# MLP phase of a fused attention and MLP kernel: one more output accumulator, one side accumulator less, an earlier load, and small vector work spread over units

## The chip, the core and the metric

The kernel runs on one core of one Trainium2 chip. The metric is the device time of one execution in microseconds (us), as a median over several runs. Profiles and traces come from single executions. A profile's span is about 1.8 us shorter than the device time of the same execution, so spans are compared with spans and times with times.

Names: TensorE is PE in profile lines, VectorE is DVE, ScalarE is ACT, GpSimd is POOL.

## The reference, cut to what matters

Part A is attention with a recurrent memory over 64 segments; part B is layer norm, two matrix products and a gelu, for each of 2048 rows. Gates mix the two.

```python
def _B_ref(x, w1, b1, w2, b2):                 # x (1, 2048, 512), w1 (512, 1376), w2 (1376, 512)
    y = _layernorm(x, axis=-1)
    h = _gelu(jnp.einsum('bsd,df->bsf', y, w1) + b1)
    return jnp.einsum('bsf,fd->bsd', h, w2) + b2
g = _sigmoid((x * gate_w).sum(-1, keepdims=True))
a = _A_ref(x, A_mem0, A_Wq, A_Wk, A_Wv, A_Wo, A_seg_len)     # the attention, unchanged here
b = _B_ref(x, B_w1, B_b1, B_w2, B_b2)
return g * a + (1 - g) * b
```

## The kernel before

The MLP comes first, then the attention. The 16 tiles of 128 rows form 8 blocks of two. The hidden width of 1376 makes 11 pieces, so the MLP is a loop over 88 units. Unit `(blk, fc)` does one up-projection (four matmuls, then a gelu on ScalarE), and the down-projection of the unit two earlier (two matmuls into two accumulators, one for each tile). Statistics, norms and gate products of later tiles run beside it on VectorE. In the last three blocks, a generator (`setup`) puts one step of the attention's first projections into each unit; these use "side" banks.

```python
    ld_x(0, 1); ld_x(1, 2)
    nc.sync.dma_start(w1_sb[:, :, 0:3 * P], w1_src[:, :, 0:3 * P])
    ...
    ld_w2(0, 4)
    nc.sync.dma_start(w1_sb[:, :, 3 * P:F], w1_src[:, :, 3 * P:F])
    ld_w2(4, FCF)
    ...                                          # rest of w2, b2, m0
    ld_x(2, 4)
    ld_x(4, 8)
    ...
    def side(shape, dtype=FP32):                 # two side banks in turn
        side_n[0] += 1
        while side_n[0] - 2 in side_todo:
            flush(dve_q)
            flush(act_q)
        return bank(5 + side_n[0] % 2, shape, dtype)

    def stats(t0, t1, act=False):                # for each tile: bn_stats, bn_aggr; then
        ...                                      # 12 small Newton steps for 1/sqrt(var + eps)
    def gates(t0, t1):                           # z = sum(x * gate_w), one instruction a tile
        ...
    def gates2(t0, t1):                          # tanh on ScalarE, then g and 1 - g on VectorE
        ...
    def up(u):                                   # hp: two banks
        hp = mps.tile([P, TB * P], FP32, tag="hp", bufs=2, name="hp")
        ...                                      # 4 matmuls, then the gelu on ScalarE
    def down(u, hg_):
        ...
            if fc == 0:
                bpt[T] = mps.tile([P, Dm], FP32, tag=f"bp{T % 3}", name="bp")    # three accumulators
            nc.tensor.matmul(bpt[T][:], lhsT=..., rhs=w2_sb[:rows, fc, :], start=(fc == 0), stop=(fc == FC - 1))
        if fc == FC - 1:                         # the first of the pair is emptied on VectorE,
            nc.vector.tensor_scalar(out=c_all[:, T, :], in0=bpt.pop(T)[:], scalar1=omg_all[:, T:T + 1], ...)
            c_q.append(T + 1)                    # the second later on ScalarE (c_act)
    ...
    for u in range(NBLK * FC):
        blk, fc = divmod(u, FC)
        T1 = (blk + 1) * TB
        pend.append((u, up(u)))
        c_act()
        if len(pend) > LAG:                      # LAG = 2
            down(*pend.pop(0))
        if T1 < NT:
            if fc == 1 or fc == 3:
                ys[fc // 2] = norm(T1 + fc // 2)
            elif fc == 4 or fc == 6:
                norm_tr(T1 + fc // 2 - 2, ys[fc // 2 - 2])   # transposes on TensorE, copy to yT on VectorE
        if blk % 2 == 0:
            G = 2 * blk
            if fc == 4 and G + 8 <= NT:
                stats(G + 4, G + 8)              # four tiles in one burst
            if fc == 7:
                gates(G, G + 4)                  # four tiles in one burst
        elif fc == 0:
            gates2(2 * blk - 2, 2 * blk + 2)
        ...
        if blk >= NBLK - 3:
            next(pre, None)                      # one step of setup
```

## Time and profile before

| | before |
|---|---|
| device time, median of 3 runs | 851.37 us (849.81 to 851.44) |
| span of the profile | 848.8 us |
| TensorE busy | 813.2 us, 96% |
| up-projection of block 2 starts | 38.36 us |
| MLP phase ends (last `c_all` eviction starts on ScalarE) | 115.20 us |

A wait line reads "who, line, waited for whom: us in total, times, longest". A timeline line reads "start, duration, engine, line, operation, tiles, shape, count", and in brackets the idle time of that engine before it and what ended it.

### The profile page before, as it was taken

What the parts mean: (1) busy time and instruction counts of PE and PEld (TensorE: products, weight loads), DVE (VectorE), ACT (ScalarE), POOL (GpSimd) and SP (SyncE); (2) the same over time, 40 slices, a digit from 0 to 9 for tenths busy, and PEclk for the clock granted to TensorE, in tenths of its full rate; (3) what the DMA queues carried; (4) which work ended last, traced back from release to release, by engine and by line L of the source; (5) the groups of instructions that cost most, each with busy time, mean ns of one, the idle gap of its engine ahead of it and who ended that gap; (6) DMA issues with size and microseconds to landing.
All of it is one profiled execution on the core that took longest, in us unless ns stands there. A gap on an engine that the chain in (4) does not pass through costs nothing.

```text
span 848.8 us, 49249 instructions
## 1 busy us (share of the span) xinstructions
PE 813.2 (96%) x22417; PEld 495.7 (58%) x22417; DVE 502.4 (59%) x1017; ACT 434.2 (51%) x1244; POOL 275.2 (32%) x625
## 2 busy tenths in 40 slices
PE   4989999999999999999999999999999999999986
PEld 2655455566656666556666665656665666656554
DVE  4555335666665666565666566666656566657553
ACT  2444454555545554555455555555454545555552
POOL 8000123333233424242424342333324342424220
PEclk8999999999999999999999999999999999999999
DMA  9890221010101010101000000101010101010000
GB/s 317 268 361 8 65 63 27 4 35 4 35 10 35 4 34 12 34 12 30 15 22 24 19 26 17 29 10 35 10 35 7 34 9 36 9 31 9 10 4 24
DMA packets 38216, 37.64 MB, mean 44 GB/s; under 512 B 13545, under 2 KB 36434, under 8 KB 36466
## 3 DMA queue, kind: packets, MB, share of 16 engines
q1 hardware_dynamic: 37874, 34.31, 12.3%
q8 instruction: 177, 2.90, 1.4%
q14 instruction: 37, 0.30, 0.1%
q0 software_dynamic: 128, 0.13, 0.1%
HBM read 26.03 MB, written 6.29 MB: 38 GB/s over the span
## 4 chain that ended last, share of the span: by engine, by line
PE 90%; DVE 6%; issue 1%; DMA 1%; SPq 1%; ACT 1%; DVEq 0%; ACTq 0%
PE b L210 34%; PE b L232 17%; PE b L221 17%; PE b L383 5%; PE hp L454 3%; PE bp L471 3%; PE b L359 2%; PE b L368 2%; PE b L660 1%; PE b L695 1%; PE b L388 1%; PE b L649 1%; DVE st L401 1%; DVE junk L422 1%; DMA Wo_sb<-in_A_x_dram 1%
## 5 line engine op out<-in xcount | busy, mean ns | idle before, releaser
L216 DVE STREAM_TRANSPOSE Tt<-b 128x512 f32<-128x512 f32 (+1 forms) x384 | 225.6, 613 | 79.1 <-PE b L210 65.4
L210 PEld LDWEIGHTS <-hT 128*32 128x32 bf16 x5120 | 134.8, 97 | 100.0 <-DVE hT L696 15.7
L232 PE MATMUL b<-Wo_sb,UTT 128*32 128x256 bf16 (+1 forms) x4736 | 162.7, 285 | 1.2 <-ACT UTT L595 0.8
L221 PE MATMUL b<-Wv_sb,hT 128*32 128x512 bf16 x2048 | 141.9, 378 | 0.0
L210 PE MATMUL b<-Wq_sb,hT 128*32 128x512 bf16 x2048 | 133.0, 379 | 1.4 <-DVE hT L696 1.4
L210 PE MATMUL b<-Wk_sb,hT 128*32 128x256 bf16 (+1 forms) x3072 | 133.4, 308 | 0.0
L232 PEld LDWEIGHTS <-UTT 128*32 128x32 bf16 x4736 | 121.3, 97 | 19.6 <-ACT UTT L595 1.5
L630 ACT CAST KT<-Tt 128x256 bf16<-128x256 f32 (+1 forms) x192 | 87.1, 476 | 53.6 <-DVE Tt L216 53.5
L581 POOL TENSOR_TENSOR Px<-E,R 128x256 bf16<-128x256 bf16 x64 | 43.1, 673 | 219.0 <-DVE R L665 219.0
L665 DVE RECIPROCAL R<-b 128x256 f32<-128x256 f32 x64 | 112.5, 1757 | 0.0
L630 POOL CAST QT<-Tt 128x512 bf16<-128x512 f32 x64 | 39.3, 614 | 192.3 <-DVE Tt L216 192.3
L595 ACT CAST UTT<-b 128x256 bf16<-128x256 f32 x256 | 76.8, 386 | 23.6 <-PE b L388 23.1
L684 ACT CAST wsb<-b 128x256 bf16<-128x256 f32 x66 | 24.6, 373 | 120.0 <-PE b L232 120.0
L653 DVE RECIPROCAL R<-b 128x64 f32<-128x64 f32 x64 | 35.6, 557 | 79.1 <-PE b L650 79.1
L630 ACT CAST QT<-Tt 128x512 bf16<-128x512 f32 x64 | 39.6, 619 | 67.6 <-DVE Tt L216 67.6
L459 ACT ACTIVATE hg<-hp,b_sb 128x256 bf16<-128x256 f32 x80 | 37.6, 473 | 54.1 <-PE hp L454 54.1
L383 PEld LDWEIGHTS <-V 32*128 32x128 bf16 x4096 | 35.2, 91 | 46.5 <-DVE Pm L655 32.4
L221 PEld LDWEIGHTS <-hT 128*32 128x32 bf16 x2048 | 49.5, 96 | 21.1
L664 ACT CAST UTT<-b 128x64 bf16<-128x64 f32 x128 | 20.9, 215 | 75.6 <-PE b L388 75.6
L454 PE MATMUL hp<-yT,w_sb 128*128 128x256 bf16 (+1 forms) x352 | 55.8, 284 | 2.5 <-DVE yT L444 2.5
L583 POOL TENSOR_TENSOR racc<-racc,R 128x320 f32<-128x320 f32 x64 | 55.6, 868 | 0.0
L471 PE MATMUL bp<-w_sb,hg 128*128 128x512 bf16 x160 | 50.0, 392 | 3.7 <-DVE c_all L474 3.7
(116 smaller groups left out, 1046.5 us busy)
## 6 DMA issues: line engine op xcount, KB each, us to landing
Wv_sb<-in_A_Wv_dram SPq DMA_DIRECT2D x4, 1024.0 KB
Wq_sb<-in_A_Wq_dram SPq DMA_DIRECT2D x4, 1024.0 KB
Wk_sb<-in_A_Wk_dram SPq DMA_DIRECT2D x4, 1024.0 KB
Wo_sb<-in_A_Wo_dram SPq DMA_DIRECT2D x2, 2048.0 KB
vd<-vt SPq DMA_DIRECT2D x32, 128.0 KB
vs<-vd SPq DMA_DIRECT2D x256, 16.0 KB
out_dram<-o SPq DMA_DIRECT2D x16, 128.0 KB
Wo_sb<-in_A_x_dram SPq DMA_DIRECT2D x1, 1024.0 KB
```

The source lines that it names most:

```text
L210: nc.tensor.matmul(bk[32 * j:32 * j + 32, 0:n], lhsT=G[:, kc, :], rhs=W5[t][:, kc, h0:h1, j, :], start=(kc == 0), stop=(kc == KC - 1), til ...
L216: nc.vector.transpose(out=Tt[:, 0:n], in_=bk[:, 0:n])
L221: nc.tensor.matmul(bk[32 * j:32 * j + 32, :], lhsT=G[:, kc, :], rhs=Wv5[:, kc, 4 * vb:4 * vb + 4, j, :], start=(kc == 0), stop=(kc == KC - ...
L232: nc.tensor.matmul(bk[32 * g:32 * g + 32, :], lhsT=ut[:, i, j, c0:c0 + 32], rhs=Wo_sb[:, 4 * i + j, d0:d1], start=(j == 0 and i < 4), stop ...
L383: nc.tensor.matmul(U[j][:, i, :], lhsT=V[q, i, :], rhs=Pt[q, i, c_main:c_main + n], start=(i == 0), stop=False, skip_group_check=True, til ...
L454: nc.tensor.matmul(hp[:rows, :], lhsT=w1_sb[:, kc, fc * P:fc * P + rows], rhs=yTs[blk][:, kc, :], start=(kc == 0), stop=(kc == KC - 1))
L471: nc.tensor.matmul(bpt[T][:], lhsT=hg_[:rows, tt * P:(tt + 1) * P], rhs=w2_sb[:rows, fc, :], start=(fc == 0), stop=(fc == FC - 1))
L581: nc.gpsimd.tensor_tensor(out=Px[:, :, 0:32], in0=E[:, :, 16:48], in1=Rr, op=ALU.mult)
L583: nc.gpsimd.tensor_tensor(out=racc[:], in0=racc[:], in1=R[:], op=ALU.add)
L595: nc.scalar.copy(out=UTT[T % 2][:, :, j, c0 + M:c0 + 40], in_=U[:])
L630: (nc.gpsimd.tensor_copy if bi == 2 else nc.scalar.copy)(out=dst, in_=Tv)
L665: nc.vector.reciprocal(out=R[:, 8 * NG:].rearrange("p (i q) -> p i q", q=32), in_=sr)
```

## The change

The intent is to take TensorE's waits out of the MLP phase. Each tile of a block and of the next gets its own accumulator, paid for with one of the two side banks. x of block 1 is loaded ahead of w2. Statistics and gates are dealt out one tile to a unit. Two smaller moves go with it: the transposes come one unit later, and `c_act` (the ScalarE eviction) runs once a block. The diff is cut, and some short lines are joined.

```diff
     nc.gpsimd.dma_start(gw_bc[:], gate_w.partition_broadcast(P))
+    ld_x(2, 4)
     ld_w2(0, 4)
 ...
-    ld_x(2, 4)
     ld_x(4, 8)
 ...
-    pools["nTt"] = 2
+    pools.update(nTt=2, nside=1)                 # side(): nside banks in turn; 2 again in the attention
 ...
-                bpt[T] = mps.tile([P, Dm], FP32, tag=f"bp{T % 3}", name="bp")
+                bpt[T] = mps.tile([P, Dm], FP32, tag=f"bp{T % 4}", name="bp")
 ...                                               # setup: one more step after each tile's eviction
             flush(act_q)
-        left_v_in(0)
+            yield
 ...
                 flush(dve_q)
+                yield
+        left_v_in(0)
 ...
-    stats(0, 2, act=True)
+    bn(0); bn(1); root_act(0, 2)
 ...
-    stats(2, 4)
+    bn(2); bn(3); newton(2, 4)
 ...
-        c_act()
+        if fc == 2:
+            c_act()
 ...
-            elif fc == 4 or fc == 6:
+            elif fc == 5 or fc == 7:               # norm_tr
 ...
         if blk % 2 == 0:
-            G = 2 * blk
-            if fc == 4 and G + 8 <= NT:
-                stats(G + 4, G + 8)
-            if fc == 7:
-                gates(G, G + 4)
-        elif fc == 0:
-            gates2(2 * blk - 2, 2 * blk + 2)
+            if fc in (2, 5, 6, 7) and T1 + 2 < NT:
+                bn(T1 + 2 + (2, 5, 6, 7).index(fc) )
+            if fc == 8 and T1 + 2 < NT:
+                newton(T1 + 2, T1 + 6)
+        elif fc in (2, 4, 6, 8):
+            T = T1 + (fc - 2) // 2
+            if T < NT:
+                gates(T, T + 1)
+        elif fc == 10 and T1 < NT:
+            gates2(T1, T1 + 4)
+        if blk == 0 and fc in (9, 10):
+            gates(fc - 9, fc - 8)
+        if blk == 1 and fc == 0:
+            gates2(0, 2)
+        if blk == 1 and fc in (1, 3):
+            gates(2 + fc // 2, 3 + fc // 2)
+        if blk == 1 and fc == 9:
+            gates2(2, 4)
```

More of the change, by code (lines that the diff above doesn't have):

```diff
@@ L195, in side @@
         side_n[0] += 1
-        while side_n[0] - 2 in side_todo:
+        n = pools["nside"]
+        while side_n[0] - n in side_todo:
             flush(dve_q)
             flush(act_q)
-        return bank(5 + side_n[0] % 2, shape, dtype)
+        return bank(5 + side_n[0] % n, shape, dtype)
     Wq5 = Wq_sb[:].rearrange("p k (h j e) -> p k h j e", h=H, j=4)
@@ L394, with bn, root_act, newton @@
     I32 = mybir.dt.int32
-    def stats(t0, t1, act=False):
-        n = t1 - t0
-        for T in range(t0, t1):
-            st = mwork.tile([P, nc.vector.BN_STATS_DIM], FP32, tag="st", bufs=4, name="st")
-            nc.vector.bn_stats(out=st[:], in_=x_all[:, T, :])
-            nc.vector.bn_aggr(out=mv_all[:, T, :], in_=st[:])
-        if act:
-            nc.scalar.activation(out=rstd_all[:, t0:t1], in_=mv_all[:, t0:t1, 1], func=ACTF.Sqrt, bias=eps_t[:], scale=1.0)
-            nc.vector.reciprocal(out=rstd_all[:, t0:t1], in_=rstd_all[:, t0:t1])
-            return
+    def bn(T):
+        st = mwork.tile([P, nc.vector.BN_STATS_DIM], FP32, tag="st", bufs=4, name="st")
+        nc.vector.bn_stats(out=st[:], in_=x_all[:, T, :])
+        nc.vector.bn_aggr(out=mv_all[:, T, :], in_=st[:])
+    def root_act(t0, t1):
+        nc.scalar.activation(out=rstd_all[:, t0:t1], in_=mv_all[:, t0:t1, 1], func=ACTF.Sqrt, bias=eps_t[:], scale=1.0)
+        nc.vector.reciprocal(out=rstd_all[:, t0:t1], in_=rstd_all[:, t0:t1])
+    def newton(t0, t1):
+        n = t1 - t0
         ve = mwork.tile([P, n], FP32, tag="ve", name="ve")
@@ L508 @@
     nc.vector.memset(eps_t[:], LN_EPS)
-    stats(0, 2, act=True)
+    bn(0)
+    bn(1)
+    root_act(0, 2)
     nc.scalar.activation(out=warm[:], in_=eps_t[:], func=ACTF.Gelu_apprx_tanh)
@@ L513 @@
     norm_tr(1, ys[1])
-    stats(2, 4)
+    bn(2)
+    bn(3)
+    newton(2, 4)
     pre = setup()
@@ L558 @@
     cw = loop.enter_context(tc.tile_pool(name="cw", bufs=2))
-    pools.update(ps=pb, sb=cw, nTt=3)
+    pools.update(ps=pb, sb=cw, nTt=3, nside=2)
     man = tc.manual_schedule()
```

## The prediction

> **What bounds the kernel now.** I read the page's busy shares and the chain that ended last first, to see which engine sets the time, then the waits of TensorE in the first 155 us, then the timelines of TensorE, VectorE and ScalarE in the stretch that the diff touches.
>
> ```profile
> span 848.8 us, 49249 instructions
> PE 813.2 (96%) x22417; PEld 495.7 (58%) x22417; DVE 502.4 (59%) x1017; ACT 434.2 (51%) x1244; POOL 275.2 (32%) x625
> ...
> PE 90%; DVE 6%; issue 1%; DMA 1%; SPq 1%; ACT 1%; DVEq 0%; ACTq 0%
> ```
>
> TensorE is busy 96% of the span and is 90% of the chain. The diff touches only the MLP phase, which ends at about 115.2 us (its last down-projections, a chain piece "PE bp L471 x6", run from 113.87 for 1.31 us). The remaining 733 us, the recurrent attention, have the same instructions before and after. So the question is how much TensorE idles before 115 us. Its waits there (window 0 to 155 us):
>
> ```profile
> PE tp L443 <- DVE y L436: 10.5, 2, 5.7
> PE bp L471 <- DVE c_all L474: 3.7, 3, 1.6
> PE hp L454 <- DVE yT L444: 2.5, 3, 1.0
> ...
> PE tp L443 <- DVE yT L444: 0.5, 1, 0.5
> ```
>
> The timeline of TensorE alone puts them in time:
>
> ```profile
> 13.71 0.59 PE L471 MATMUL bp<-w_sb,hg 128*128 128x512 bf16 x2
> 19.12 0.61 PE L443 MATMUL tp<-ident,y 128*128 128x128 bf16 x4 [4.81 <-DVE y L436]
> ...
> 30.75 0.38 PE L471 MATMUL bp<-w_sb,hg 128*128 128x512 bf16 x1 [1.20 <-DVE c_all L474]
> ...
> 49.66 0.61 PE L454 MATMUL hp<-yT,w_sb 128*128 128x256 bf16 x4 [1.00 <-DVE yT L444]
> ...
> 53.83 0.38 PE L471 MATMUL bp<-w_sb,hg 128*128 128x512 bf16 x1 [1.61 <-DVE c_all L474]
> ...
> 72.73 0.61 PE L454 MATMUL hp<-yT,w_sb 128*128 128x256 bf16 x4 [1.00 <-DVE yT L444]
> ...
> 76.91 0.38 PE L471 MATMUL bp<-w_sb,hg 128*128 128x512 bf16 x1 [0.88 <-DVE c_all L474]
> ```
>
> Three kinds. The first, 4.81 us, is TensorE waiting for the normed rows of tiles 2 and 3. The waits on c_all (1.20, 1.61, 0.88) are a down-projection that needs a third accumulator while VectorE has not emptied the old one. The waits on yT (1.00, 1.00) are the next block's first up-projection. Two smaller ones (a pair of down-projections at 40.54 and 63.61 shows 0.73 in place of 0.59) add 0.13 each. After 77 us there is none until the phase ends. What lies behind each is in the timeline of VectorE:
>
> ```profile
> 14.48 0.69 DVE L401 BATCH_NORM_STATS2 st<-Wo_sb 128x6 f32<-128x512 bf16 x1 [6.63 <-DMA Wo_sb<-in_A_x_dram]
> ...
> 49.18 0.42 DVE L444 COPY yT<-tp 128x512 bf16<-128x512 bf16 x1
> 49.52 0.68 DVE L422 SCALAR_TENSOR_TENSOR junk<-Wo_sb,gw_bc 128x512 bf16<-128x512 bf16 x1
> ...
> 53.02 0.75 DVE L474 TENSOR_SCALAR c_all<-bp,omg_all 128x512 bf16<-128x512 f32 x1
> ```
>
> The first wait is a transfer: x of tiles 2 and 3 lands at 14.48, behind all of w1 and w2; statistics and Newton steps follow until 18.65. The later ones are bursts: between 43.60 and 49.27 VectorE does four statistics and one Newton chain without a break, so the copy of yT comes at 49.18; then four gate products stand before c_all at 53.02.
>
> **What the Trainium skill says.** "TensorE: Matmul & The Clock Gate", Part 1, says that the array runs at half rate until it was busy for a window of about 3.4 us, and falls back after an idle one. The trace agrees: one unit (four up-matmuls, two down-matmuls) has a pitch of 1.71 us after the 4.81 us wait (19.52 to 21.23) and of 0.87 us later (24.40 to 25.27), and the granted clock reads 0.50 from 17 to 23 us. The same page (Part 1, "Architectural detail") calls the queues of ScalarE and VectorE strict FIFO; the bursts above show it, as the yT copy waits behind Newton steps that it does not need. "DMA: Bandwidth & Descriptors", "Queues, rings and completion order", says that an engine consumes descriptors in ring order; it fits x(2,4) landing last. "Perfetto Trace Analysis", "Optimization Strategy", says that consistent bubbles can mean too few buffers; the c_all waits, once in every second block, are of that kind.
>
> **The change, part by part.** *(a) x of tiles 2 and 3 ahead of w2.* Its 256 KB now come after 640 KB (x of tiles 0, 1 and the first w1 part), not after some 3,000 KB. From the DMA rates by slice (about 87, 177, 332 GB/s in the first three slices of 2.9 us) I estimate a landing at 7.8 us. VectorE is free at 7.85 (it has just copied the second yT), and from the first statistic to the norm took 18.65 - 14.48 = 4.17 us, so norm(2) is ready to start at 12.0, not 18.65. The rest of w1 is pushed back by 256 KB at some 370 GB/s (the mean of the two slices there, 388 and 351), about 0.7 us: it landed at 11.40 (TensorE waited for it 0.83), so now at 12.1.
>
> *(b) The new wait in block 0.* The statistic of tile 4 now stands in VectorE's queue at unit 2, ahead of norm(3). Its x is in the 512 KB that still follow the weights: the bytes ahead are the same as before, so it lands 512 KB / 400 GB/s = 1.3 us after 14.48, at 15.9 (estimate). From there by durations of the trace (pitch of one statistic with its aggregate 0.80, norm 0.40, copy 0.40, Newton 2.35, gate 0.74): statistic 4 to 16.7, norm(3) 17.1, copy(2) 17.5, statistics 5 and 6 19.1, copy(3) 19.5, statistic 7 20.3, Newton 22.7, gates of tiles 0 and 1 to 24.2. TensorE meanwhile, at half rate up to about 13.3 and 0.87 a unit after, with 0.22 for each transpose group, finishes block 0 at 20.4 and unit 13 at 22.95. Then it stops: the tanh for the gates sits in ScalarE's FIFO after the gelu of unit 11, waits for z until 24.2, and holds back the gelu of unit 12, whose hp buffer unit 14 needs. 24.2 + 0.2 (tanh) + 0.47 (gelu) = 24.9: a wait of 1.95 us. This chain from x(4,8), not TensorE, sets the time here; a TensorE up to 1.95 us later changes nothing.
>
> Remaining block 1: eight units of 0.87 and two transpose groups, 7.4 us, and 0.4 for the second transpose, since VectorE, still catching up with the gates of tiles 2 to 7, copies yT(4) only at 29.85. Block 2 starts at 24.9 + 7.4 + 0.4 = 32.7. Before, it started at 38.36. **Gain so far 5.7 us**: 4.81 of wait, 2.1 of half clock after it (4.2 us at half rate) and 1.20 of c_all wait go, about 0.7 for w1 and the two new waits come.
>
> *(c) Four accumulators and spread work, blocks 2 to 7.* With four banks a block's two accumulators are needed again only two blocks on, 10 us after their last matmul, so the eviction is never in the way: 0.13 + 1.61 + 0.13 + 0.88 = 2.75 us go. VectorE's work in an even block is now 0.75 + 2 x 0.40 + 4 x 0.80 + 2 x 0.42 + 2.35 = 7.9 us in a block of 10.0 (11 x 0.87 + 2 x 0.22); the copy of the second yT stands behind three statistics, not behind Newton, and is done three units before it is needed. An odd block has 0.75 + 0.80 + 4 x 0.74 + 0.84 + 0.33 = 5.7 us. So the two yT waits of 1.00 go as well. **4.75 us.**
>
> *(d) One side buffer in place of two.* Costs a bank (4 + 2 + 1 + 1 = 8). The added yields put one unit, 1.30 us in this stretch (77.55 to 78.85), between the last matmul into the side bank and the first into the next; the eviction takes 0.71 on VectorE or 0.58 on ScalarE. Setup needs 31 steps and a last one, of 33 units. 0 us. The late copy of VL (1.04 us on GpSimd) ends about when the phase does and is first needed in the attention of step 0: 0 us.
>
> Sum: 5.7 + 4.75 = 10.4 us. 851.4 - 10.4 = **841.0 us**.
>
> **The rivals.** *Everything hides:* if TensorE never waited after the change, the upper bound is 4.81 + 2.1 + 1.20 + 4.75 = 12.9 us, 838.5. For it speaks an x(4,8) that lands near 14; against it the equal bytes ahead of it. *The tile-4 statistic waits longer:* if Wv's transfers, issued from 8.68, share the rings with x(4,8), it lands at 18 and each us is lost directly: 843 to 844. Against it speaks ring order. *The side bank becomes a wait:* if each of seven evictions came 0.5 late, 3.5 us are lost, 844.5; against it the 1.30 us unit. *VectorE becomes the bound* in even blocks: at 7.9 of 10.0 us it would need work that I have missed; one us per block would give 847. *The clock does not rise at 13.3* because of the 0.8 us hole for w1: up to 1.7 us of TensorE time, but inside the 1.95 of slack, so nothing.
>
> **Range and chances.** The removable idle time is 12.9 us, 1.5%, so over 2% (below 834.3) would need something in the attention, where nothing changed. The rivals that cost lie between 1 and 6 us, and the runs before spread by 1.6. Eight in ten: 838 to 845. Faster by over 2%: 0.03; within 2%: 0.95; slower: 0.02.
>
> **What would show it.** Right: no wait on y of 4.8 us in TensorE's list, and the granted clock not back at 0.50 near 17 to 23 us; one wait of 1 to 2 us for ScalarE near 23 us; VectorE idle until about 16 us on a transfer of x; no c_all or yT waits of 0.9 or more from 33 us on; the phase's last down-projection ending near 104.8 in place of 115.2; attention as long as before within 1 us. Wrong: a new wait on the side bank between 65 and 100 us, repeated waits of TensorE on yT in even blocks, or an attention part that differs by more than 2 us.

## More of the kernel before

Line numbers of the kernel before and of the changed one differ (the up-projection is L454 before and L456 after).

The end of the MLP phase is this line (timeline of ScalarE, kernel before):

```profile
115.20 0.69 ACT L479 ACTIVATE c_all<-bp,omg_all 128x512 bf16<-128x512 f32 x1 [0.83 <-PE bp L471]
```

## The result

| | before | changed |
|---|---|---|
| device time, median of 4 runs each | 851.40 us | 838.42 us (837.94 to 839.50) |
| ratio changed / before | | 0.9849 (0.9828 to 0.9870) |
| span of the profile | 848.8 us | 836.5 us |
| up-projection of block 2 starts | 38.36 us | 32.33 us |
| MLP phase ends | 115.20 us | 103.73 us |

A ratio is the mean time of one kernel's fast runs over the mean of the other's fast runs of the same rounds, so it is not quite the ratio of the medians. The gain is 13.0 us (1.5%), within the predicted range and at its fast end; 10.4 us were predicted. It is even just past the prediction's "upper bound" (838.5, TensorE never waiting), although TensorE still waited; the part on why the prediction was right says how.

The page of the changed kernel: busy shares, then the chain that ended last.

```profile
PE 810.3 (97%) x22404; PEld 495.3 (59%) x22417; DVE 502.4 (60%) x1019; ACT 434.2 (52%) x1245; POOL 274.4 (33%) x625
...
PE 93%; DVE 3%; DMA 1%; SPq 1%; issue 1%; ACT 1%; DVEq 0%; ACTq 0%
```

VectorE's busy time is the same, 502.4 us. Its share of the chain fell from 6% to 3%: the same work stands in other places.

TensorE's waits in the first 155 us of the changed kernel (those in the attention are left out):

```profile
PE tp L445 <- DVE y L438: 5.7, 1, 5.7
...
PE hp L456 <- DMA w_sb<-in_B_w_dram: 0.7, 1, 0.7
PE tp L445 <- DVE yT L446: 0.5, 1, 0.5
PE hp L456 <- DVE yT L446: 0.5, 1, 0.5
PE hp L456 <- ACT hg L461: 0.5, 1, 0.5
```

The first line is the start of the kernel, which was there before as half of the 10.5 us on `y`. The other half, 4.81 us, is gone, and so are all waits on `c_all` and the two of 1.00 on `yT`. Two small ones are new: 0.7 on w1, and 0.5 on a gelu of ScalarE. Here is where they lie (timelines of TensorE, VectorE and ScalarE of the changed kernel):

```profile
12.21 1.03 PE L456 MATMUL hp<-yT,w_sb 128*128 128x256 bf16 x4 [0.71 <-DMA w_sb<-in_B_w_dram]
...
24.94 0.60 PE L456 MATMUL hp<-yT,w_sb 128*128 128x256 bf16 x4 [0.51 <-ACT hg L461]
```

```profile
16.14 0.69 DVE L399 BATCH_NORM_STATS2 st<-Wo_sb 128x6 f32<-128x512 bf16 x1 [3.44 <-DMA Wo_sb<-in_A_x_dram]
```

```profile
24.32 0.20 ACT L427 ACTIVATE th_all<-z_all 128x2 f32<-128x2 f32 x1 [1.49 <-DVE junk L424]
24.43 0.82 ACT L461 ACTIVATE hg<-hp,b_sb 128x256 bf16<-128x256 f32 x2
...
103.73 0.69 ACT L481 ACTIVATE c_all<-bp,omg_all 128x512 bf16<-128x512 f32 x1 [0.83 <-PE bp L473]
```

VectorE stands for 3.44 us until x of tile 4 lands at 16.14. From there statistics, Newton steps and two gate products run on it without a break until 24.3; the tanh on ScalarE waits for the second gate, and the two gelus behind it come late. The last line is the end of the MLP phase.

The 12.3 us between the two spans split into 6.0 up to the start of block 2, 5.4 in blocks 2 to 7, and 0.8 after the MLP phase.

### The profile page after: what moved, and what is told of

It reads as the page before. It is cut to its first block, busy times and chain, and to the rows that moved or that the text cites. A ratio compares the mean times of both kernels' runs of the same rounds, so it can differ in the third digit from the quotient of the medians.

```text
span 836.5 us, 49240 instructions
## 1 busy us (share of the span) xinstructions
PE 810.3 (97%) x22404; PEld 495.3 (59%) x22417; DVE 502.4 (60%) x1019; ACT 434.2 (52%) x1245; POOL 274.4 (33%) x625
## 3 DMA queue, kind: packets, MB, share of 16 engines
q1 hardware_dynamic: 37874, 34.31, 12.3%
## 4 chain that ended last, share of the span: by engine, by line
PE 93%; DVE 3%; DMA 1%; SPq 1%; issue 1%; ACT 1%; DVEq 0%; ACTq 0%
PE b L211 35%; PE b L233 18%; PE b L222 17%; PE b L384 5%; PE hp L456 4%; PE bp L473 4%; PE b L360 2%; PE b L369 2%; PE b L681 2%; PE b L716 1%; PE b L389 1%; PE b L670 1%; DMA Wo_sb<-in_A_x_dram 1%; PE b L320 1%; PE b L373 0%
## 5 line engine op out<-in xcount | busy, mean ns | idle before, releaser
L717 DVE CAST hT<-b 128x32 bf16<-128x32 f32 x63 | 12.1, 192 | 61.8 <-PE b L716 61.8
```

## The experiments

The theory put to the test had four claims: (1) after the change, the chain from the landing of x of tiles 4 to 7 over VectorE to the tanh sets when block 2 starts; (2) waits do not add up, since one that is removed uncovers the next; (3) it is the order of VectorE's work, not the number of accumulators, that made the `c_all` waits of blocks 2 to 7; (4) the single side bank is free because of the added steps. The rivals were additive waits, TensorE alone as the bound of the head, and the fourth bank as the cure. Claim (3) goes against the attribution in the prediction.

All results in one table. "x at 4" is when VectorE starts the statistic of tile 4 after waiting for its x. The column "blocks 2-7" is the end of the MLP phase minus the start of block 2, all from the profiles. Times and ratios of the experiments are of 4 or 5 runs beside 9 runs of the kernel before on the same chip (of the changed kernel, 4 beside 4); every output of the experiments was correct.

| run | x at 4 | block 2 starts | MLP ends | blocks 2-7 | time, us | ratio to before (95%) |
|---|---|---|---|---|---|---|
| before | | 38.36 | 115.20 | 76.84 | 851.40 | |
| changed | 16.14 | 32.33 | 103.73 | 71.40 | 838.42 | 0.9849 (0.9828 to 0.9870) |
| e1_x_early_only | 15.98 | 34.38 | 111.24 | 76.86 | 847.90 | 0.9962 (0.9948 to 0.9975) |
| e2_x_late | | 36.44 | 107.83 | 71.39 | 842.51 | 0.9902 (0.9887 to 0.9917) |
| e3_three_acc | 16.00 | 33.11 | 104.91 | 71.80 | 841.08 | 0.9884 (0.9869 to 0.9899) |
| e4_four_acc_bursts | 16.31 | 33.99 | 110.13 | 76.14 | 844.96 | 0.9929 (0.9916 to 0.9943) |
| e5_gates_in_gap | | 31.36 | 102.76 | 71.40 | 834.96 | 0.9817 (0.9803 to 0.9830) |
| e6_w1_split | 16.71 | 32.79 | 104.19 | 71.40 | 838.68 | 0.9855 (0.9840 to 0.9870) |
| e7_both | | 29.90 | 101.30 | 71.40 | 835.68 | 0.9823 (0.9809 to 0.9836) |
| e8_x48_late | 19.57 | 35.63 | 107.03 | 71.40 | 840.45 | 0.9878 (0.9863 to 0.9893) |
| e9_no_added_steps | 15.89 | 32.07 | 105.08 | 73.01 | 839.69 | 0.9868 (0.9850 to 0.9885) |
| e10_gap_three_acc | 16.05 | 31.29 | 103.08 | 71.79 | 837.20 | 0.9844 (0.9827 to 0.9860) |
| after_again | 16.89 | 32.97 | 104.37 | 71.40 | 837.43 | 0.9844 (0.9828 to 0.9860) |
| before_again | | 38.44 | 115.29 | 76.85 | 850.52 | 0.9998 (0.9984 to 1.0012) |

### The early load alone (e1)

```diff
 # kernel before
+    ld_x(2, 4)
     ld_w2(0, 4)
 ...
-    ld_x(2, 4)
     ld_x(4, 8)
```

> The kernel before with the early load of x for tiles 2 and 3 alone. The MLP phase (start of the last c_all eviction on ScalarE) ended at 115.2 before and 103.7 after. Theory of chained waits (a wait removed is partly replaced by the next one in line): the 4.81 wait on y goes, but the block of four statistics now waits for x of tiles 4 to 7 at about 16 us, Newton ends near 21.7, the copy of the second yT near 22.2, and new waits of TensorE of about 1.2 (yT) and 1.7 (c_all) us come before 28 us; phase end near 110.9, time near 847. Rival, additive waits: the wait and the cold stretch after it are worth 4.81 + 2.1 = 6.9 us; phase end near 108.3, time near 844.5.

The MLP phase ended at 111.24, 0.3 from the theory and 2.9 from the additive rival. TensorE in this run (timeline, up to 30 us):

```profile
22.18 1.03 PE L454 MATMUL hp<-yT,w_sb 128*128 128x256 bf16 x4 [2.67 <-DVE yT L444]
...
26.77 0.38 PE L471 MATMUL bp<-w_sb,hg 128*128 128x512 bf16 x1 [0.55 <-DVE c_all L474]
```

The 4.81 us wait is gone, but the burst of four statistics now waits for the next x, and the copy of the second `yT` stands behind it. The size of each new wait was off (2.67 and 0.55, not 1.2 and 1.7), their sum by 0.3. That the end came so near is in part luck: the theory had no cold stretch, but after the 2.67 the next two units of TensorE took 1.67 and 1.56 us (22.18 to 23.85 to 25.41) in place of 0.87. Blocks 2 to 7 took as long as before, 76.86.

### The early load taken back out (e2)

```diff
 # changed kernel
-    ld_x(2, 4)
     ld_w2(0, 4)
 ...
+    ld_x(2, 4)
     ld_x(4, 8)
```

> The changed kernel with the load of x for tiles 2 and 3 put back behind the weights; four accumulators, one side bank and the spread VectorE work stay. Chained waits: the wait on y of 4 to 5 us and the cold stretch to about 23 us come back, but VectorE is no later than TensorE afterwards, so the wait for ScalarE near 24 us vanishes; block 2 starts near 35.4 (32.3 in the changed kernel), phase end near 106.8, time near 841.5. Additive rival: the whole 6.9 us come back; phase end near 110.6, time near 845.3.

The 4.90 us wait on `y` came back, and no wait for ScalarE was left, as the theory said. Block 2 started at 36.44 and not at 35.4. One unit (0.87) left out of the expectation would explain most of that, but the record does not show its sum. The early load is worth 4.1 us at the end of the MLP phase, between the two expectations (3.1 and 6.9) and nearer to the first.

### Three accumulators with spread work (e3), four with bursts (e4)

```diff
 # e3: changed kernel
-    pools.update(nTt=2, nside=1)
+    pools.update(nTt=2, nside=2)
-                bpt[T] = mps.tile([P, Dm], FP32, tag=f"bp{T % 4}", name="bp")
+                bpt[T] = mps.tile([P, Dm], FP32, tag=f"bp{T % 3}", name="bp")
 # e4: e1, with four accumulators, nside=1 and the added steps; stats() and gates() in bursts as before
```

> The changed kernel with three output accumulators and two side banks as before; early x and the spread VectorE work stay. If the bursts on VectorE made the c_all waits, and not the number of banks, the eviction is prompt: about 0.13 us lost at each of four block boundaries without side work and about 0.9 more at the boundary of blocks 0 and 1, where VectorE lags; phase end near 105.2, time near 839.8. Rival, the fourth bank is what removed those waits: 2.75 us in blocks 2 to 7 and 1.2 in block 1 come back; phase end near 107.7, time near 842.4.

> The kernel before with early x, four accumulators and one side bank (with its added steps), but statistics, Newton and gates in bursts as before. Theory: the c_all waits go, the yT waits of about 1.0 to 1.2 in blocks 3 and 5 stay, and in part of the c_all waits' place TensorE waits for a gelu that stands behind the tanh on ScalarE (about 0.75 in block 3, about 1.0 in block 1); phase end near 107.8, time near 842.5. Rival, the banks alone take all the c_all waits and nothing takes their place: only the yT waits are lost against the changed kernel, phase end near 105.7, time near 840.4. Waits on the side bank would appear between 73 and 108 us on TensorE; none expected.

Together with e1 and the changed kernel these are the four corners of one comparison, all with the early load. Time of blocks 2 to 7:

| | bursts | spread |
|---|---|---|
| three accumulators, two side banks | 76.86 (e1) | 71.80 (e3) |
| four accumulators, one side bank | 76.14 (e4) | 71.40 (changed) |

Spreading is worth 5.06 us with three accumulators and 4.74 with four; the fourth accumulator is worth 0.40 us with spread work and 0.72 with bursts. The rival, the fourth bank as the cure, is wrong for blocks 2 to 7 by these numbers. ("Spread" is the whole new order of the loop, the later transposes and the single `c_act` included; no run takes these apart.)

The device times give the bank more. The medians of the same four corners are 847.90, 841.08, 844.96 and 838.42: spreading is worth 6.5 to 6.8 us, the bank 2.7 to 2.9. Of that the profiles show 1.1 to 1.2 up to the end of the MLP phase (111.24 to 110.13, 104.91 to 103.73); where the rest lies is not shown.

Both kernels that kept the bursts kept their losses; in e4 they only changed their names (TensorE, timeline):

```profile
22.49 1.04 PE L455 MATMUL hp<-yT,w_sb 128*128 128x256 bf16 x4 [2.82 <-DVE yT L445]
45.16 0.61 PE L455 MATMUL hp<-yT,w_sb 128*128 128x256 bf16 x4 [1.00 <-DVE yT L445]
48.56 0.60 PE L455 MATMUL hp<-yT,w_sb 128*128 128x256 bf16 x4 [0.62 <-ACT hg L460]
67.12 0.61 PE L455 MATMUL hp<-yT,w_sb 128*128 128x256 bf16 x4 [1.00 <-DVE yT L445]
70.52 0.40 PE L222 MATMUL b<-Wv_sb,GL 128*32 128x512 bf16 x4 [1.20 <-DVE hT L488]
89.81 0.40 PE L211 MATMUL b<-Wk_sb,GL 128*32 128x512 bf16 x4 [0.27 <-DVE Tt L217]
```

The `c_all` waits are gone. In their place TensorE waits for a gelu behind the tanh (0.62, expected 0.75), and for the single side bank, whose eviction on VectorE stands behind the gates (1.20) and behind a copy of yT (0.27). None of the latter were expected, nor the 2.82 at 22.49 (after which, as in e1, two units ran slow), so e4 ended at 110.13 and not at 107.8: the theory had the direction and missed 2.3 us. The rival was further off (105.7).

In block 1 the fourth accumulator matters more: in e3 TensorE waited there for `c_all`, because VectorE still lags (timeline of TensorE, e3). About 0.9 us was expected for it:

```profile
25.50 0.38 PE L473 MATMUL bp<-w_sb,hg 128*128 128x512 bf16 x1 [2.52 <-DVE c_all L476]
```

### What sets the head (e5, e6, e7, e8, and the changed kernel again)

```diff
 # e5: changed kernel, block 0 only
-            if fc == 1 or fc == 3:
+            if blk == 0:
+                if fc == 1:
+                    ys = [norm(T1), norm(T1 + 1)]
+            elif fc == 1 or fc == 3:
 ...
+            if blk == 0 and fc == 2:
+                for T in range(4):
+                    gates(T, T + 1)              # in the gap before x of tile 4 lands
+            if blk == 0 and fc == 9:
+                gates2(0, 4)
+            if blk == 0 and fc == 5:
+                bn(T1 + 2)                       # was at fc == 2
 ...                                              # the later gates and gates2 of tiles 0 to 3 are removed
 # e6: changed kernel
+    nc.sync.dma_start(w1_sb[:, :, 3 * P:5 * P], w1_src[:, :, 3 * P:5 * P])
     ld_w2(0, 4)
-    nc.sync.dma_start(w1_sb[:, :, 3 * P:F], w1_src[:, :, 3 * P:F])
+    nc.sync.dma_start(w1_sb[:, :, 5 * P:F], w1_src[:, :, 5 * P:F])
 # e7: e5 and e6 together
 # e8: changed kernel, ld_x(4, 8) moved behind the first quarter of Wv
 # after_again: the changed kernel as it is
```

> The changed kernel with the second norm and the gates of tiles 0 to 3 moved ahead of the statistic of tile 4, into the 3.4 us in which VectorE waits for x of tiles 4 to 7; that statistic comes after the first yT copy. Theory: the chain from the landing of x(4,8) over statistics, Newton and gates to the tanh sets block 1, so without it block 2 is set by TensorE: start 31.7 if the clock rises near 16.4 as in the changed kernel's profile, 30.4 if it rises near 13 (32.3 in the changed kernel); phase end 103.1 or 101.8, time 837.8 or 836.5; no wait for ScalarE before 30 us. Rival, TensorE alone (half clock, weights) sets the head: block 2 still starts near 32.3, phase end 103.7.

> The changed kernel with the first two slices of the rest of w1 loaded ahead of w2, so that the 0.7 us hole of TensorE at 11.5 us closes. Theory of the chain from x(4,8): TensorE only arrives earlier at unit 14 and waits there longer (1.2 us in place of 0.5, or 2.6 if the clock rises early); phase end 103.7, time as the changed kernel, 838.4. Rival, TensorE sets the head: the 0.7 us are won, phase end 103.0, time 837.7.

> Both edits: gates in VectorE's gap and the first slices of w1 ahead of w2. Theory: now the hole counts, so this gains 0.7 over the gates edit alone although the w1 edit alone gained nothing; phase end 102.4 (late clock) or 101.1 (early clock), time 837.1 or 835.8, the fastest so far. Rival: the sum of the two single gains.

> The changed kernel with x of tiles 4 to 7 loaded behind the first quarter of Wv (1 MB, about 2.5 us at 410 GB/s). Theory of the chain: each us of that landing is a us of the end, so VectorE's wait ends near 18.6, block 2 starts near 34.8, phase end 106.2, time 840.9. Rival, the landing has slack: phase end below 104.5, time below 839.2.

> The changed kernel again, to see what one profile leaves to chance. Theory of the chain: whenever the clock rises (13 or 16.4 us), block 2 starts at 32.3 plus what x(4,8) lands later than 16.1, because the wait for ScalarE takes up the difference (0.5 with a late, up to 2.5 with an early rise); phase end 103.5 to 104.3. Rival: with an early rise block 2 starts 1.2 or more us earlier.

The profile of the changed kernel run again shows claim (1) more clearly than any edit. In it TensorE already ran at full rate at 13.04 (0.61 for four matmuls of the up-projection; in the first profile they still took 1.06 at 13.89). It gained nothing by that:

```profile
13.04 0.61 PE L456 MATMUL hp<-yT,w_sb 128*128 128x256 bf16 x4 [1.52 <-DMA w_sb<-in_B_w_dram]
18.48 0.38 PE L445 MATMUL tp<-ident,y 128*128 128x128 bf16 x4 [0.71 <-DVE yT L446]
25.58 0.60 PE L456 MATMUL hp<-yT,w_sb 128*128 128x256 bf16 x4 [1.50 <-ACT hg L461]
```

```profile
16.89 0.69 DVE L399 BATCH_NORM_STATS2 st<-Wo_sb 128x6 f32<-128x512 bf16 x1 [3.47 <-DMA Wo_sb<-in_A_x_dram]
```

x of tile 4 landed 0.75 later (second fence, VectorE), and block 2 started 0.64 later. In the five profiles with four accumulators and the changed kernel's chain, block 2 starts 16.06 to 16.19 us after that landing: 32.33 - 16.14, 32.97 - 16.89, 32.79 - 16.71 (e6), 35.63 - 19.57 (e8), 32.07 - 15.89 (e9). In e8 the landing came 3.43 us later (2.5 were estimated) and the MLP phase ended 3.30 later. These lines of e8, VectorE and then TensorE, read as those above do:

```profile
19.57 0.69 DVE L398 BATCH_NORM_STATS2 st<-Wo_sb 128x6 f32<-128x512 bf16 x1 [6.13 <-DMA Wo_sb<-in_A_x_dram]
```

```profile
28.24 0.60 PE L455 MATMUL hp<-yT,w_sb 128*128 128x256 bf16 x4 [1.46 <-ACT hg L460]
```

e5 takes four gates out of the chain and into the gap. The wait for ScalarE is gone, block 2 starts at 31.36, and the time is 834.96, the lowest median; the rival (32.3) is wrong, though a part of the 0.97 us may be the clock, which was up at about 15.7 and not 16.4. The profile is of e5's slowest run (837.62), so most of its runs gained more than the profile shows. e6 gained nothing in time, as the theory had it, and TensorE stood longer (1.72 and 1.49). But its means failed: the hole for w1 was not closed but moved, since w2's first part now came late:

```profile
10.99 1.01 PE L474 MATMUL bp<-w_sb,hg 128*128 128x512 bf16 x2 [0.40 <-DMA w_sb<-in_B_w_dram]
```

In e7 the same wait was 0.69. So e7 does not test what it was meant to test. Its profile ends the MLP phase 1.46 before e5's, but its clock was up at 11.15 and e5's only at about 15.7, and its median is 0.7 above e5's. Which of the two is faster stays unclear; both beat the changed kernel.

### The added steps (e9), and three accumulators without the lag (e10)

```diff
 # e9: changed kernel, setup()
             flush(act_q)
-            yield
 ...
                 flush(dve_q)
-                yield
 # e10: e5 with nside=2 and bp{T % 3}
```

> The changed kernel with one side bank but without the added steps, so that the first matmul into the side bank for the next tile comes one unit after the last one of the tile before. Theory: the two evictions on ScalarE stand behind that unit's gelu and end about 1.5 us after the unit begins, while TensorE is there after 0.87: a wait of about 0.6 each on the vt copy; the VectorE evictions (0.72) just fit, with one or two waits of 0.1 to 0.3; phase end near 105.2, time near 840. Rival: the steps are idle, phase end 103.7, no wait on the side bank.

> The version with the gates in VectorE's gap, with three accumulators and two side banks. Theory: once VectorE does not lag, the fourth accumulator is worth about 0.13 at each of five block boundaries; block 2 starts between 30.5 and 31.5 depending on the clock, blocks 2 to 7 take 71.8 (71.4 with four), phase end 102.3 to 103.3, no listed c_all wait over 0.3. Rival: the fourth bank is what removed the c_all waits; 2.75 come back in blocks 2 to 7, phase end 105 or more.

e9: blocks 2 to 7 took 73.01 in place of 71.40, so the steps are worth 1.6 us; the expected phase end (105.2 for 103.7) says 1.5. TensorE waited on the side bank where it was said it would:

```profile
70.16 0.40 PE L222 MATMUL b<-Wv_sb,GL 128*32 128x512 bf16 x4 [0.44 <-ACT vt L282]
76.33 0.40 PE L211 MATMUL b<-Wq_sb,GL 128*32 128x512 bf16 x4 [0.67 <-ACT vt L282]
```

e10: blocks 2 to 7 took 71.79 (71.8 expected), so the fourth accumulator's worth of 0.4 us there is seen a second time. The rival (105 or more) is wrong. One part of the expectation failed: a `c_all` wait of 1.52 stood at 23.68, where none over 0.3 was expected, since VectorE's Newton steps still ended late:

```profile
23.68 0.38 PE L473 MATMUL bp<-w_sb,hg 128*128 128x512 bf16 x1 [1.52 <-DVE c_all L476]
```

This probably hides a loss before block 2. TensorE was at full rate by 10.34 in this profile and only at about 15.7 in e5's, yet block 2 started as late (31.29 and 31.36). By device time e10 is 2.2 us slower than e5 (837.20 and 834.96), far more than 0.4 (the profiles are of e10's fastest run and e5's slowest).

### The attention (before_again)

No edit: the kernel before as it is.

> The kernel before once more, for a second profile: of the 13 us gained, 11.5 lie in the MLP phase of the two profiles and about 0.8 in the attention (733.6 us from the end of the MLP phase to the end before, 732.8 and 732.2 in the two profiles of the changed kernel), where the instructions are the same. If that difference is chance of a single profile, this one shows an attention between 732.2 and 733.3. If the attention is really longer in the kernel before, it shows 733.6 or more. The MLP phase ends at 115.2 plus or minus 1 in both cases, and block 2 to the end of block 7 takes 76.8.

The attention (end of the MLP phase to the end of the span) took 735.1 us, above the 733.6 that had been set as the mark of a real difference. In the ten profiles with spread work (e2, e3, e5 to e10 and the changed kernel twice) it took 732.0 to 733.8; in the four with bursts (before twice, e1, e4) 733.6 to 735.1: means of 732.8 and 734.3, but ranges that touch. The differences sit in a few of the 64 steps, by 0.2 to 1.1 us each, and the largest of the kernel before is at step 42. There TensorE stood before a matmul in the kernel before with nothing the profile names:

```profile
586.79 0.22 PE L383 MATMUL b<-Px,V 32*128 32x32 bf16 x7 [0.33 <-issue]
```

The changed kernel has no such gap at that step, but e3, with spread work, has one of 0.31, so the spreading alone does not remove it. Since the attention's instructions are the same, the cause could be where they lie in the instruction stream, but no run tests that. About 1.5 us of the gain stays unexplained here.

## Why the prediction was right, and where it was not

**(a) The early x.** Right. Statistic 2 started at 8.06 (7.85 predicted), norm(2) at 12.29 (12.0), and the up-projection that needs the rest of w1 at 12.21 (12.1). The wait of 4.81 us went. One reading was wrong without effect: the 0.83 on w1 was a wait of the weight loads (PEld); the matmul lost only about 0.12 there (11.41, due at 11.29).

**(b) The chain from x(4,8).** Right, and the best part of the working: landing 16.14 (15.9), tanh at 24.32 (24.2), TensorE on again at 24.94 (24.9). The wait for ScalarE was 0.51 and not 1.95, for a reason the rivals named: the clock rose near 16.4 and not near 13.3. (The cause that the rival gave, the hole for w1, is not borne out: the rerun had a longer hole, 1.52, and was at full rate right after it.) That used up the slack and cost nothing. The rerun, with an early clock and a wait of 1.50, and e8 show that the landing sets the time. One term was mis-sized: 0.4 us for the second transpose group, "since VectorE, still catching up with the gates of tiles 2 to 7, copies yT(4) only at 29.85". It was copied at 28.91, so there was no wait. The step used durations in a row where pitches belong: a norm lasts 0.40, but the next instruction starts after 0.32. From `c_all` at 24.91 to the copy this makes 4.00 us, where the prediction's durations (0.75 + 2 x 0.40 + 4 x 0.74) sum to 4.51; the rest of the 0.94 cannot be traced, since its sum is not shown.

```profile
24.91 0.75 DVE L476 TENSOR_SCALAR c_all<-bp,omg_all 128x512 bf16<-128x512 f32 x1
25.58 0.40 DVE L438 TENSOR_SCALAR y<-Wo_sb,mv_all,rstd_all 128x512 bf16<-128x512 bf16 x1
25.90 0.68 DVE L424 SCALAR_TENSOR_TENSOR junk<-Wo_sb,gw_bc 128x512 bf16<-128x512 bf16 x1
...
28.91 0.42 DVE L446 COPY yT<-tp 128x512 bf16<-128x512 bf16 x1
```

The Trainium skill says so in "Perfetto Trace Analysis", "Optimizing Scalar/DVE Operations": part of an instruction's profiled time overlaps the next one. This trace agrees, with 0.08 us for the norm. The terms listed beside the head's gain of 5.7 do not add up either: 4.81 + 2.1 + 1.20 - 0.7 - 1.95 - 0.4 is 5.1; 6.0 were measured.

**(c) Blocks 2 to 7.** The direction was right, the sum of 4.75 too small (5.44), and the attribution wrong. The mis-sized term is the value of a wait. A wait costs more than the idle time that its line gives: the down-projection at 53.83 was due one pitch (0.22) after the one at 51.84, so at 52.06, and 1.77 us were lost where the line says 1.61. Taken that way the waits in blocks 2 to 7 are 1.17 + 1.77 + 1.17 + 1.05 and twice 0.13, 5.4 in all, which is the gain. The wrong attribution is the sentence "With four banks a block's two accumulators are needed again only two blocks on ... so the eviction is never in the way: ... 2.75 us go". e3 and e4 show that the banks were worth 0.4 to 0.7 there; spreading the work, which moves VectorE's bursts away from the eviction, did the rest. That the sum came near in spite of this is luck: the change did both things at once.

**(d) The side bank.** Right for the changed kernel: no wait on it. e9 shows that this rests on the added steps (1.6 us without them), and e4 that it rests on the spreading too.

**The attention** was taken to be equal within 1 us. In the first two profiles it was (0.8), but the means over all profiles differ by 1.5. Of the 2.6 us between the predicted 10.4 and the measured 13.0, the head gave 0.3 (6.0 for 5.7) and term (c) 0.7; the remaining 1.6 lie outside the MLP phase of the two profiles, with the cause open. These are also why the "upper bound" of 12.9 was none: it summed idle times, which understate waits, and took the attention as fixed.

## What to carry to other kernels

When an accumulator is emptied late, look first at what stands ahead of the eviction in that engine's queue: dealing a burst out over several units took away 5 us of waits in blocks 2 to 7 that looked like a lack of banks, and the extra bank took 0.4 to 0.7 there. Check the device times as well: they put the bank at 2 to 3 us in all. A wait that is removed is worth only the distance to the next thing in line, so follow the chain from the next landing transfer before adding up savings, and then put work that depends on nothing into the gap in front of that landing (e5, 0.9817 of the time before). For hand reckoning, chain instructions on VectorE by pitch and not by duration, and take a TensorE wait as about 0.16 us more than its idle time.

## What the Trainium skill lacked or had wrong

- "TensorE: Matmul & The Clock Gate", Part 1: the fall back to half rate is put after an idle window of about 3.4 us. In e1 a wait of 2.67 us was enough (four matmuls took 1.03 after it, against 0.60 at full rate), in e4 one of 2.82; in e3 one of 2.52 was not (0.38 for a matmul right after).
- The same part gives the moment of the rise as good to 500 ns, and also calls it variable from run to run. Two profiles of the changed kernel, with first transposes at 5.70 and 5.54, were at half rate at 14.74 in one and at full rate at 13.04 in the other.
- No page says that the granted clock of a profile can read full through the cold start; the same part only warns in general that the throttle's events in a trace can be unreliable. In this slice of the kernel before (time, length, busy times of PE, PEld, DVE, ACT and POOL, PEclk, DMA share, GB/s) it reads 1.00, while the twelve matmuls around it (7.91 to 10.43) took 0.21 us each and not 0.11 as later:

```profile
9.00:10.00 1.00, 1.00 (x7) 0.67 (x5) 0.00 (x0) 0.62 (x2) 0.95 (x8) 1.00 1.04 401
```

- "Perfetto Trace Analysis", "Optimization Strategy": regular bubbles can mean too few buffers. Here that was the smaller part: with three accumulators and spread work blocks 2 to 7 took 71.80 us, with four and bursts 76.14.
- No page says by how much an idle time of TensorE understates a wait: about 0.16 us each here.
- "DMA: Bandwidth & Descriptors" gives no spread of a landing: the same load, with the same bytes ahead of it, was used by VectorE from 15.89 to 16.89 us in seven profiles (e1, e3, e4, e9, e10 and the changed kernel twice).
